# The experts' stage: 1 MB weight loads issued from Pool's queue instead of SyncE's

## The chip, the cores and the metric

The kernel runs on one core of a Trainium2 chip. The core has five engines with an instruction queue each: PE (TensorE, matrix products), DVE (VectorE), ACT (ScalarE), POOL (GpSimd) and SP (SyncE, which here only issues DMAs). DMAs that SP issues go through one hardware queue, those that Pool issues through a software queue. The metric is the device time of one execution in microseconds, lower is better.

## The reference

Three layers in a row, on a batch of 8 with 8 heads: an attention between 512 positions and 32 states per batch and head; a mixture of 8 experts, in which each of the 4352 tokens goes to one expert; and a feed-forward layer with float64 weights.

```python
def _moe_ref(x, expert_emb, tau, w1, w2):
    ...
    for e in range(E):
        mask = expert_idx == e
        h = np.maximum(x[mask] @ w1[e], 0.0)
        out[mask] = gate_w[mask, None] * (h @ w2[e])

def _moe2_ref(x, w_in, w_out, alpha):
    h = x @ w_in
    g = np.maximum(h, 0.0) + alpha * np.minimum(h, 0.0)
    return (g @ w_out).astype(np.float32)
```

D = 512, the experts' hidden width is 1024, that of the feed-forward layer 2048.

## The kernel before

Three stages follow each other: attention with routing, the experts (`moe`), the feed-forward layer (`ffn`). The profile's experts' stage lies between about 165 and 610 us.

`moe` goes through slots of 128 tokens, sorted by expert, one `step(s)` for each. The order of all instructions is written out by hand: each engine runs its own in the order in which the code emits them. Values are kept as a high and a low float16 part, so a product is three. A step does this:

- Token preparation, two steps ahead: `g_load` (L1035, Pool) gathers 128 rows by index into `xg`; `x_prep` (L138 to L140, Pool) scales them and splits them into `xs`; SP issues a DMA transpose of `xs` into `xTt` (L1041).
- First product: `mm1` (L1050, PE, 24 matmuls) reads `xTt`. `relu` splits the result into `hs` (L194 on ACT, L195 on DVE), and SP issues the DMA transpose `hT<-hs` (L1058).
- Second product: `mm2` of the step before (L1063, PE, 24 matmuls) reads `hT`. PE runs mm1(s+1) and then mm2(s), so `hT` has the time of mm1(s+1) to arrive.
- Result: `y_top` and `y_out` scale and split it into `ys` (L1070 to L1073 and L130 on DVE, L127 on ACT), Pool copies two indices (L1079) and scatters the rows to memory (L1083, `y_nat<-ys`).
- Weight swaps: where the next slot belongs to another expert (read from a table, so under branches), SP loads 2 MB of new weights into `st` in four DMAs (`swap`, L1101), and ACT and DVE convert them.

Beside this the stage prepares the feed-forward weights, which are float64. `d_load` (L1109 to L1115) brings 16 pieces of 1 MB, as pairs of int32, into `d64`, one buffer (bufs=1). `d_parts` turns a piece into float32 with three DVE instructions (`decode_ops`, L146 to L148) and then calls `d_load` for the next piece, which has to wait until the last of the three, L148, has read the buffer. The pieces are decoded in steps 2, 4, 6, 7, 8, 10, 12, 14, 18, 20 and so on to 32. `step` spreads these operations: the first runs inside `y_out`, the rest goes to `left` and runs in the next step, after `relu` and ahead of `x_prep`:

```python
            while left:
                left.pop(0)()
            ops = [op for f in work[s] for op in f()]
            ...
            if s + 2 < MS:
                x_prep(s + 2)
            y_top(s - 1)
            ...
            y_out(s - 1, fill)
            left.extend(ops)
```

Of the kernel before, what the change touches and what calls it, by code (L numbers as in the profile page):

```python
# [22 lines left out]
def tile_attn_moe_ffn(ctx, tc, x, xt, state, statet, embt, tau, w1, w2, w_in, w_out, alpha, out):  # L23


    nc = tc.nc
# [981 lines left out]
    def moe(st, winh, winl, wf, yq, yps, scp, pm, tables, order, gates):  # L1008
# [99 lines left out]
        def d_load(c):  # L1108
            d64[c] = mp.tile([128, 1024, 2], I32, tag="d64", bufs=1, name="d64")  # L1109
            if c < 8:  # L1110
                src = w_in32[(c // 2) * 128:(c // 2 + 1) * 128, (c % 2) * 2048:(c % 2 + 1) * 2048]
                nc.sync.dma_start(d64[c].rearrange("p a b -> p (a b)"), src)
            else:
                src = w_out32[(c - 8) * 256:(c - 7) * 256, :].rearrange("(k p) n -> p k n", p=128)
                nc.sync.dma_start(d64[c].rearrange("p (k a) b -> p k (a b)", k=2), src)  # L1115

        def d_parts(c):
            cs = slice((c % 8) * 1024, (c % 8 + 1) * 1024)
            ops = decode_ops(wf[:, cs], d64[c])
            if c < 15:  # L1120
                ops.append(lambda: d_load(c + 1))
            return ops
# [6 lines left out]
        d64, work = {}, {s: [] for s in range(MS)}  # L1129
# [27 lines left out]
        y_top(0)  # L1157
        y_out(0)
        d_load(0)

        left = []
# [410 lines left out]
```

## Time and profile before

| | us |
|---|---|
| median of 3 runs | 1306.46 (1304.74 to 1307.47) |
| the profiled execution | 1298.37 |
| its span | 1296.7 |
| PE busy in the span | 1209.7 (93%) |
| DVE / ACT / POOL busy in the span | 807.2 / 566.4 / 359.7 |
| DMA through SP's queue (q1) | 117.30 MB, 38.3% of 16 engines' span |
| DMA through Pool's queue (q0) | 29.49 MB, 7.8% |

The profile is of one execution. A row of the time line gives the start in us from the span's start, the duration in us, the engine (SPq is SP's queue of issues), the line of the code, the operation, what it writes and reads, how many instructions were merged into the row, and in brackets how long the engine had been idle and who ended that wait. An issuing row tells how long the issue took, not the transfer. "issue" as a releaser means that the profile shows nothing that was waited for.

### The profile page before, as it was taken

How to read it: one execution, taken by the hardware profiler on the slowest of the kernel's cores; microseconds unless marked ns; L12 is line 12 of the kernel's file. 1: busy time of each engine (PE TensorE's matmuls, PEld its weight loads, DVE VectorE, ACT ScalarE, POOL GpSimd, SP SyncE). 2: the span in 40 equal slices, each digit the busy share in tenths (PEclk: the TensorE clock that was granted, in tenths of full speed). 3: DMA queues.
4: the chain of work that ended last, by engine and by line, in shares of the span. 5: the costliest groups of instructions: out<-in, count | busy, mean ns of one | idle time of the engine just before them, and what ended most of it. 6: DMA issues, size and time to landing. Idle time of an engine off the chain costs nothing. (4 is left out here: it accounts for less than half of the span.)

```text
span 1296.7 us, 21099 instructions
## 1 busy us (share of the span) xinstructions
PE 1209.7 (93%) x7520; PEld 688.1 (53%) x7520; DVE 807.2 (62%) x1640; ACT 566.4 (44%) x1045; POOL 359.7 (28%) x421
## 2 busy tenths in 40 slices
PE   8888799898988898988899999999999999999997
PEld 5555444343333343433345666666666666666664
DVE  5898866656777776745986645645555553654543
ACT  5965532225474545443544333333433433333343
POOL 2345445544436544543302002020010202001010
PEclk9987999999989999999899999999999999999999
DMA  9984777999899999884102010020100202010000
GB/s 289 307 244 141 214 172 178 196 183 244 203 260 216 271 226 224 208 172 92 34 1 58 9 33 33 1 66 1 42 25 1 66 1 57 9 18 33 1 33 17
DMA packets 221648, 148.48 MB, mean 115 GB/s; under 512 B 174014, under 2 KB 190526, under 8 KB 220480
## 3 DMA queue, kind: packets, MB, share of 16 engines
q1 hardware_dynamic: 210976, 117.30, 38.3%
q0 software_dynamic: 10240, 29.49, 7.8%
q8 instruction: 61, 1.00, 0.3%
q14 instruction: 83, 0.68, 0.2%
q10 hardware_dynamic: 288, 0.02, 0.0%
HBM read 80.13 MB, written 28.40 MB: 84 GB/s over the span
## 5 line engine op out<-in xcount | busy, mean ns | idle before, releaser
L1386 PE MATMUL bk<-woh,arena 128*128 128x512 f16 x1088 | 391.8, 380 | 4.4 <-ACT arena L1366 2.8
L1386 PEld LDWEIGHTS <-arena 128*128 128x128 f16 x1632 | 158.5, 98 | 120.2 <-ACT arena L1366 3.1
L1386 PE MATMUL bk<-wol,arena 128*128 128x512 f16 x544 | 206.7, 380 | 0.0
L1293 POOL DMA_INDIRECT out_dram<-arena,fr x34 | 36.2, 1065 | 588.5 <-ACT arena L1391 552.0
L1446 DVE SCALAR_TENSOR_TENSOR arena<-bk,sg,arena 128x256 f32<-128x256 f32 (+1 forms) x128 | 59.7, 467 | 219.8 <-PE bk L1440 215.8
L1366 ACT CAST arena<-arena 128x512 f16<-128x512 f32 (+1 forms) x144 | 85.0, 590 | 188.7 <-DVE arena L1371 188.6
L1063 PE MATMUL yp<-w2h,hT 128*128 128x512 f16 x576 | 138.6, 396 | 29.4 <-DMA hT<-hs 21.8
L1448 ACT ACTIVATE arena<-pm,sg 128x256 f32<-128x256 f32 (+1 forms) x192 | 88.3, 461 | 158.1 <-PE pm L1440 156.8
L1063 PEld LDWEIGHTS <-hT 128*128 128x128 f16 x864 | 82.8, 100 | 137.4 <-DMA hT<-hs 35.8
L1050 PE MATMUL hp<-w1h,xTt 128*128 128x512 f16 x576 | 136.9, 389 | 15.4 <-DMA xTt<-xs 9.6
L1050 PEld LDWEIGHTS <-xTt 128*128 128x128 f16 x864 | 85.0, 99 | 124.5 <-issue 16.1
L1440 PEld LDWEIGHTS <-wS 128*128 128x128 f16 x1152 | 108.6, 98 | 52.7
L1440 PEld LDWEIGHTS <-winh 128*128 128x128 f16 x1024 | 98.0, 98 | 49.8 <-issue 2.1
L1370 DVE TENSOR_TENSOR arena<-arena 128x512 f16<-128x512 f32 (+1 forms) x144 | 94.1, 658 | 17.8 <-ACT arena L1366 17.1
L1371 DVE SCALAR_TENSOR_TENSOR arena<-arena,alpha_sb 128x512 f32<-128x512 f32 (+1 forms) x144 | 102.7, 714 | 2.9 <-ACT arena L1406 2.6
L127 ACT ACTIVATE ys<-yp,ym 128x512 f16<-128x512 f32 x38 | 26.0, 684 | 171.8 <-DVE ym L1072 157.5
L1440 PE MATMUL pm<-ysum,wS 128*128 128x256 f16 (+1 forms) x768 | 99.6, 266 | 0.0
L1083 POOL DMA_INDIRECT y_nat<-ys,pos x38 | 39.4, 1037 | 209.8 <-issue 135.4
L1440 PE MATMUL bk<-yT,winh 128*128 128x256 f16 (+1 forms) x512 | 86.5, 266 | 0.0
L1050 PE MATMUL hp<-w1l,xTt 128*128 128x512 f16 x288 | 68.4, 379 | 0.0
L1063 PE MATMUL yp<-w2l,hT 128*128 128x512 f16 x288 | 68.1, 378 | 0.1
L161 ACT ACTIVATE junk<-st 128x1024 bf16<-128x1024 f32 x56 | 59.1, 1056 | 19.4 <-SPq L1097 5.8
(318 smaller groups left out, 1904.4 us busy)
## 6 DMA issues: line engine op xcount, KB each, us to landing
st<-in_w_dram SPq DMA_DIRECT2D x64, 512.0 KB
X<-in_x_dram SPq DMA_DIRECT2D x32, 256.0 KB
d<-in_w_in_dram SPq DMA_DIRECT2D x8, 1024.0 KB
d<-in_w_out_dram SPq DMA_DIRECT2D x8, 1024.0 KB
xs_all<-xrow SPq DMA_DIRECT2D x7, 1056.0 KB
xT<-in_xt_dram SPq DMA_DIRECT2D x7, 1024.0 KB
xs_all<-xrow SPq DMA_DIRECT2D x2, 528.0 KB
xT<-in_xt_dram SPq DMA_DIRECT2D x2, 512.0 KB
```

Of the source, the lines that this page charges most:

```text
L161: nc.scalar.activation(out=junk, in_=W[i][0][:, c, :], func=AF.Square, accum_out=fsq[i][:, c:c + 1])
L1050: nc.tensor.matmul(hp[s][c], lhsT=xTt[s][:, q + k, :], rhs=wt[:, k, c * 512:(c + 1) * 512], start=(i == 0 and k == 0), stop=(i == 2 and k ...
L1063: nc.tensor.matmul(yp[s], lhsT=hT[s][:, q + k, :], rhs=wt[:, k, :], start=(i == 0 and k == 0), stop=(i == 2 and k == KE - 1))
L1083: nc.gpsimd.indirect_dma_start(out=y_nat[:], out_offset=bass.IndirectOffsetOnAxis(ap=pos[:, s:s + 1], axis=0), in_=ys[:].bitcast(I32), in_ ...
L1293: nc.gpsimd.indirect_dma_start(out=out, out_offset=bass.IndirectOffsetOnAxis(ap=fr[g][:, t, 2:3].bitcast(U32), axis=0), in_=src, in_offset ...
L1366: nc.scalar.copy(slot[G[g, m]][:, 0, 0:n], h)
L1370: tt(d[:, 1, 0:n], h, d[:, 0, 0:n], sub)
L1371: return [lambda: nc.vector.scalar_tensor_tensor(h, in0=h, scalar=alpha_sb[:, m:m + 1], in1=h, op0=ALU.mult, op1=ALU.max), hi, lo]
L1386: nc.tensor.matmul(ps, lhsT=slot[G[g, m]][:, lg, t * 128:(t + 1) * 128], rhs=wo[lw][:, m, :], start=(m == order[0] and i == 0), stop=(m == ...
L1440: nc.tensor.matmul(ps, lhsT=a, rhs=b, start=(i in (1, 2, 5) and j == 0), stop=(j == len(ops) - 1), skip_group_check=True)
L1446: nc.vector.scalar_tensor_tensor(d, in0=ps, scalar=sc, in1=d, op0=ALU.mult, op1=add)
L1448: nc.scalar.activation(out=d, in_=ps, func=AF.Copy, scale=sc)
```

## The change

The two lines that issue the 16 loads of `d64` name another engine's queue. Nothing else in the code is changed; the place in the code at which a load is called stays.

```diff
@@ -1109,10 +1109,10 @@
             d64[c] = mp.tile([128, 1024, 2], I32, tag="d64", bufs=1, name="d64")
             if c < 8:
                 src = w_in32[(c // 2) * 128:(c // 2 + 1) * 128, (c % 2) * 2048:(c % 2 + 1) * 2048]
-                nc.sync.dma_start(d64[c].rearrange("p a b -> p (a b)"), src)
+                nc.gpsimd.dma_start(d64[c].rearrange("p a b -> p (a b)"), src)
             else:
                 src = w_out32[(c - 8) * 256:(c - 7) * 256, :].rearrange("(k p) n -> p k n", p=128)
-                nc.sync.dma_start(d64[c].rearrange("p (k a) b -> p k (a b)", k=2), src)
+                nc.gpsimd.dma_start(d64[c].rearrange("p (k a) b -> p k (a b)", k=2), src)
```

The order of SP before the change, at the eleventh load (the one of the time line's 407.26 us): the load, the transpose of the tokens, under a branch four loads of weights, the transpose of the hidden tile.

```order
686 L1115 DMA d_5297<-in_w_out_dram 128x2x1024
687 L1095 UNCONDITIONAL_BRANCH
688 L1105 UNCONDITIONAL_BRANCH
689 L1041 DMA_TRANSPOSE xTt_2266<-xs_2264 128x8x128
690 L113 TENSOR_LOAD tab
691 L1097 COMPARE_AND_BRANCH
```

After the change SP's rows at that place begin with the transpose.

```order
676 L1095 UNCONDITIONAL_BRANCH
677 L1105 UNCONDITIONAL_BRANCH
678 L1041 DMA_TRANSPOSE xTt_2266<-xs_2264 128x8x128
679 L113 TENSOR_LOAD tab
680 L1097 COMPARE_AND_BRANCH
```

The load has gone from between the branches; what follows on SP stands in the same order as before.

Pool before the change, from the preparation of the tokens (`xs_2264`) that this transpose reads, to the store and the gather that follow.

```order
378 L138 TENSOR_TENSOR xg_2261<-xg_2261 128x512
379 L139 CAST xs_2264<-xg_2261 128x512
380 L140 TENSOR_TENSOR xs_2264<-xg_2261,xs_2264 128x512
381 L1079 COPY ys_2274<-ids 128x2
382 L1090 UNCONDITIONAL_BRANCH
383 L1095 UNCONDITIONAL_BRANCH
384 L1105 UNCONDITIONAL_BRANCH
385 L1097 UNCONDITIONAL_BRANCH
386 L1095 UNCONDITIONAL_BRANCH
387 L1105 UNCONDITIONAL_BRANCH
388 L1083 DMA y_nat<-ys_2274,pos 4352x528
389 L1035 DMA xg_2258<-xs_all,idx 128x528
```

Pool after the change, the same stretch.

```order
392 L1115 DMA d_5297<-in_w_out_dram 128x2x1024
393 L1095 UNCONDITIONAL_BRANCH
394 L1105 UNCONDITIONAL_BRANCH
395 L138 TENSOR_TENSOR xg_2261<-xg_2261 128x512
396 L139 CAST xs_2264<-xg_2261 128x512
397 L140 TENSOR_TENSOR xs_2264<-xg_2261,xs_2264 128x512
398 L1079 COPY ys_2274<-ids 128x2
399 L1083 DMA y_nat<-ys_2274,pos 4352x528
400 L1035 DMA xg_2258<-xs_all,idx 128x528
```

The load, and with it the wait for DVE's L148, now stands on Pool ahead of the three instructions that make `xs_2264`, which SP's transpose waits for; the copy, the store and the gather follow. It is so at fifteen of the sixteen loads; the first has no decode ahead of it.

## Rows read from the trace of the kernel before

**Rows 1.** Busy time by stage (stretch, us, each engine, PE clock, DMA share, GB/s)

```profile
165.00:610.00 445.00, 400.11 (x1795) 174.41 (x1793) 299.03 (x536) 198.70 (x301) 215.23 (x225) 0.97 0.91 205
```

**Rows 2.** Waits of PE, 165 to 610 us (total, times, longest)

```profile
PE yp L1063 <- DMA hT<-hs: 21.8, 10, 4.5
PE hp L1050 <- DMA xTt<-xs: 9.6, 5, 4.1
```

**Rows 3.** Time line of DVE, 402 to 413 us

```profile
403.88 2.03 DVE L147 SCALAR_TENSOR_TENSOR wf<-d,c_top,wf 128x1024 int32<-128x1024 int32 x1 [1.48 <-DVEq L1095]
405.95 1.28 DVE L148 SCALAR_TENSOR_TENSOR wf<-d,c_sh,wf 128x1024 int32<-128x1024 int32 x1
...
409.03 0.75 DVE L130 SCALAR_TENSOR_TENSOR ys<-yp,ym,ys 128x512 f16<-128x512 f32 x1 [0.64 <-ACT ys L127]
```

**Rows 4.** Time line of SP's issues, 195 to 520 us

```profile
199.08 1.87 SPq L1058 DMA_TRANSPOSE hT<-hs  x1
...
300.96 0.36 SPq L1112 DMA_DIRECT2D d<-in_w_in_dram  x1
301.97 1.62 SPq L1041 DMA_TRANSPOSE xTt<-xs  x1
...
382.06 0.41 SPq L1115 DMA_DIRECT2D d<-in_w_out_dram  x1
382.64 1.25 SPq L1041 DMA_TRANSPOSE xTt<-xs  x1
385.70 3.68 SPq L1101 DMA_DIRECT2D st<-in_w_dram  x4
390.93 3.57 SPq L1058 DMA_TRANSPOSE hT<-hs  x1
...
407.26 0.40 SPq L1115 DMA_DIRECT2D d<-in_w_out_dram  x1
407.84 1.26 SPq L1041 DMA_TRANSPOSE xTt<-xs  x1
411.87 3.28 SPq L1058 DMA_TRANSPOSE hT<-hs  x1
...
507.17 1.29 SPq L1041 DMA_TRANSPOSE xTt<-xs  x1
```

**Rows 5.** Time line of PE, 195 to 520 us

```profile
203.49 3.63 PE L1063 MATMUL yp<-w2h,hT 128*128 128x512 f16 x16
...
259.27 5.31 PE L1063 MATMUL yp<-w2h,hT 128*128 128x512 f16 x16 [3.67 <-DMA hT<-hs]
...
318.26 5.16 PE L1063 MATMUL yp<-w2h,hT 128*128 128x512 f16 x16 [4.46 <-DMA hT<-hs]
...
397.72 3.63 PE L1063 MATMUL yp<-w2h,hT 128*128 128x512 f16 x16 [2.91 <-DMA hT<-hs]
...
413.65 1.18 PE L1050 MATMUL hp<-w1h,xTt 128*128 128x512 f16 x4 [0.17 <-DMA xTt<-xs]
...
421.45 3.63 PE L1063 MATMUL yp<-w2h,hT 128*128 128x512 f16 x16 [0.92 <-DMA hT<-hs]
...
513.98 3.62 PE L1050 MATMUL hp<-w1h,xTt 128*128 128x512 f16 x16
```

**Rows 6.** Time line of POOL, 399 to 414 us

```profile
401.87 1.05 POOL L138 TENSOR_TENSOR xg<-xg 128x512 f32<-128x512 f32 x1
...
403.68 1.16 POOL L140 TENSOR_TENSOR xs<-xg,xs 128x512 f16<-128x512 f32 x1
...
410.56 1.03 POOL L1083 DMA_INDIRECT y_nat<-ys,pos  x1 [4.60 <-DVE ys L130]
411.89 0.98 POOL L1035 DMA_INDIRECT xg<-xs_all,idx  x1 [0.30 <-issue]
```

**Rows 7.** POOL's gathers and its one plain DMA (ns min/median/max, first and last start)

```profile
L1035 POOL DMA_INDIRECT xg<-xs_all,idx x40: 946/982/1034, 156.4 to 607.1; - x40
L281 POOL DMA_DIRECT2D xs_all<-srow x1: 822/822/822, 12.7 to 12.7; - x1
```

## The prediction

> **What bounds the kernel now.** I went from the page to the stage, then to its waits, then to one step of it on five engines. In the experts' stage TensorE is busy for 400.1 of 445 us [rows 1], so time there is TensorE's, and only what makes TensorE wait costs anything. The table of waits names what it waits for: ten times the transposed hidden tile `hT` (21.8 us) and five times the transposed tokens `xTt` (9.6 us) [rows 2]. Both are DMA transposes that SP issues, one after the other, in a fixed order. So the change matters through two questions: when SP can issue `xTt` and `hT`, and how long they then travel.
>
> The step with the load at 407.26 shows how tight this is. On VectorE the last decode, L148, ends at 405.95 + 1.28 = 407.23 and frees the buffer [rows 3]. SP, held until then, issues the load at 407.26, `xTt` at 407.84 and `hT` at 411.87, when VectorE has finished the hidden tile [rows 3, 4]. TensorE waits 0.17 us for that `xTt` until 413.65 and 0.92 us for that `hT` until 421.45 [rows 5]. `xTt` behind the load thus travels 5.8 us, `hT` 9.6 us. Pool in that step prepares the tokens from 401.87 to 403.68 + 1.16 = 404.84 and then sits idle for 4.60 us before it issues the store [rows 6]: the preparation is early and hidden.
>
> **What the change takes away.** On SP, 16 issues of about 0.4 us and the wait for L148 ahead of them [rows 4]. This is worth little by itself, as `xTt`, next on SP, still has to wait, now for Pool. On SP's DMA queue, 1 MB ahead of `xTt`. What does a transpose cost with nothing ahead? The `hT` issued at 199.08 is in use at 203.49: 4.4 us [rows 4, 5]. `xTt` is half as large; I take 3.5 us, bounded by 4.4 above and about 3 below (half of the 4.4 would be movement at most, an estimate), and 5.8 if it goes on meeting other traffic.
>
> **What it adds on Pool.** The load now stands ahead of the token preparation L138 to L140, and waits for L148. Costs from that moment: Pool's DMA starts late after a wait, as the store does (wait over at 409.03 + 0.75 = 409.78 [rows 3], start at 410.56 [rows 6]): 0.78 us. Then the issue: 0.82 us for the one plain DMA that Pool issues, 0.95 to 1.03 for the 40 gathers [rows 7]; I take 1.0, as the load has 128 rows like a gather. Then the preparation, 2.97 us (401.87 to 404.84). `xTt` goes out at 407.23 + 0.78 + 1.0 + 2.97 + 0.05 = 412.0 instead of 407.84: 4.2 us later, and with 3.5 us instead of 5.8 to travel it lands 1.9 us later. Fifteen loads stand so; the first has no decode ahead of it.
>
> Who feels it? Ten of the fifteen have several us until TensorE wants `xTt`, or belong to the next paragraph. Five are tight. In the step shown nothing is left; in the last of the five `xTt` was issued at 507.17, landed by the same 5.8 us at 513.0, and TensorE began with it, without a wait, at 513.98 [rows 4, 5]: 1.0 us left. With 0.9 left on average, five steps lose 1.0 each: **+5.0 us**.
>
> `hT` stands behind `xTt` on SP. SP needs 1.25 us to issue `xTt` and 1.8 us of branches and table reads (382.64 + 1.25 to 385.70 [rows 4]; 1.55 from the last weight load to `hT`). With 1.6, `hT` could go at 412.0 + 1.25 + 1.6 = 414.9, 3.0 us later than now. But its 9.6 us of travel are a collision: Pool issues the gather at 411.89, 0.02 us after `hT` [rows 4, 6], and the two share the DMA engines; without it 4.4 us are enough. After the change store and gather follow the preparation at once (412.5 and 413.8), about 1 us ahead of `hT`, and should mostly be through. I take 5.8 us, between 4.4 and 9.6: `hT` lands at 420.7. TensorE, 2 us late from `xTt`, wants it 24 matmuls later, at 16 in 3.63 us: 415.5 + 5.4 = 420.9. So the `hT` waits of these steps go: four, the first 3.67 us (until 259.27), with 0.92 in the step shown; 6.4 us together. The first also slowed TensorE: the 16 matmuls after it took 5.31 us where 16 take 3.63 [rows 5], 1.7 us more. **-8.1 us**.
>
> **Three loads with a weight swap behind them.** In three steps SP issues 2 MB of the next expert's weights between `xTt` and `hT`. There the 4 us are not absorbed: load at 382.06, `xTt` 382.64, weights 385.70 to 389.38, `hT` 390.93, for which TensorE waits 2.91 us until 397.72 [rows 4, 5]. With `xTt` at 382.06 + 4.8 = 386.85, weights and `hT` go out 4.1 us later, on the same queue in the same order, so TensorE starts 4.1 us later. Its wait becomes 7.0 us, longer than the 3.67 us that was followed by slow matmuls, which adds 1.7: +5.8. In the first of the three the load goes out at 300.96 and `xTt` only at 301.97, after a preparation that overlapped the decode [rows 4]; the new time, 300.96 + 4.8 = 305.8, is 3.8 us later, less up to 0.9 as the overlap ends, and the wait of 4.46 us already has the slow matmuls (5.16 [rows 5]): +2.9. The third I put at +1.8, an estimate from the first, since its preparation overlaps the decode too and SP is held up there by a swap ahead of the load as well. **+10.5 us**.
>
> **Sum.** 5.0 - 8.1 + 10.5 = +7.4 us. The profiled execution took 1298.37 us (span 1296.7), so 1305.8 for such a one. The median of the runs shown, 1306.46, lies 8.1 above it; carried over, 1306.46 + 7.4 = **1314 us**. The later store, gather and 1 MB landing cost nothing by my reading: their results are used one or two steps later, and a step is 48 matmuls, 10.9 us at 16 in 3.63.
>
> **Rivals.** *Faster.* The collision goes (-8.1) and the lateness is absorbed. For this speaks that Pool's preparation and VectorE's decode would no longer overlap: L147 took 2.03 us in the step shown, under the preparation, and L148, an instruction of the same form, 1.28 [rows 3], so the decode would end up to 0.8 us sooner. If `xTt` travels 3.0 us, the five steps lose (4.2 - 0.8 - 2.8 - 0.9, under zero) nothing. It decides if the three swap steps also lose less than 2 us each: -8.1 + 3 = -5, 1301 us. Against it: those three waits are a plain chain on SP. Chance 0.23.
>
> *No change.* SP saves its issues, Pool's idle 4.60 us swallows the preparation, and the three swap steps cost what the collision gives back: 1306 us. The Trainium skill supports this outcome (DMA: Bandwidth & Descriptors, section "Issuing engines are not separate DMA queues"): DMAs run on the same 16 engines whoever issues them, so moving an issue saves only the sequencer's own time. By that the sum would be nil, as SP's 16 issues are off the path. Chance 0.17.
>
> *Much slower.* Packets of Pool's queue between those of a transpose stretch it, as the gather does now (9.6 us against 4.4). If load tail, store and gather now do that to `xTt`, it travels 5.8 us again and lands 4.2 later: five steps lose 3.3 each, 16.5, and the `hT` waits stay (no -8.1): 16.5 + 10.5 = +27, 1333 us. Half of that is as likely as all. Chance 0.15.
>
> *Starved issue.* If VectorE holds up Pool while it issues, 1.0 us becomes 1.0 plus a VectorE instruction, 0.75 (L130) to 2.03 us (L147) [rows 3]. Over the five tight steps and three swap steps that is 6 to 16 us more: 1320 to 1330. The 40 gathers, all within 0.95 to 1.03 us beside a busy VectorE [rows 7], speak against it. The Trainium skill warns of it (SBUF — State Buffer, section "Who interferes with whom"): a DMA from Pool's queue can stall because VectorE starves its descriptor generation, and one from SP cannot. By the gathers' rows, this case's trace does not agree so far. Chance 0.07.
>
> **Chances.** My forecast, +3 to +14 us (1309 to 1321), 0.38. A measurement of this kernel tells about 0.2% (2.6 us) from no change. Faster 0.23, within 0.2% 0.17, slower 0.38 + 0.15 + 0.07 = 0.60. The range leaves out about one in ten on each side: 1298 to 1329.
>
> **What would show it.** Right: `xTt` about 4 us later after L148 in each of the 15 steps, Pool idle before the load and not before the store, waits for `xTt` up by some 5 us, waits for `hT` down except in the three swap steps, where they grow. Wrong: `xTt` at its old place, or waits for `hT` as long as now in the other steps; a Pool issue much over 1 us; or `xTt` travelling 5.8 us although the load is off its queue.

## The result and the profile after

| | before | after |
|---|---|---|
| median of 4 runs | 1305.6 us (1303.17 to 1307.47) | 1320.99 us (1318.75 to 1327.64) |
| ratio, 95% interval | | 1.0127 [1.0084, 1.0171] |
| profiled execution, its span | 1298.37, 1296.7 | 1323.19, 1321.5 |

The change makes the kernel 1.3% slower: 15.4 us between the medians, where +7.4 was forecast. The time lies inside the range, the sign is right, the size is about double.

The traffic moved as the diff says: the page's part on the queues has 100.52 MB through SP's queue (117.30 before) and 46.27 MB through Pool's (29.49).

The waits of PE after, from 165 to 640 us (total, times, longest), beside [rows 2]:

```profile
PE yp L1063 <- DMA hT<-hs: 36.2, 9, 9.8
PE hp L1050 <- DMA xTt<-xs: 10.1, 6, 3.4
PE yp L1063 <- ACT hs L194: 8.1, 1, 8.1
...
PE yp L1063 <- ACT ys L127: 2.2, 1, 2.2
```

The third row is an `hT` wait too. The view names the releaser that came last by its records, and ACT's part of `hs` was long done: the matmuls in question start at 407.82, the moment at which an `hT` lands (below). The fourth is of the same kind: its matmuls start at 375.23, and the `hT` of 363.51 lands 11.7 us after its issue. Before there were two such by their place, the first matmul that reads a new `hT`, which the prediction's 21.8 left out; from the same view of the kernel before:

```profile
PE yp L1063 <- DVE w2l L130: 4.9, 1, 4.9
...
PE yp L1063 <- ACT ys L127: 2.3, 1, 2.3
```

So PE waited 46.5 us for `hT` where it was 29.0, and for `xTt` 10.1 where it was 9.6. The tokens, which go out late, cost almost nothing where they are used; the hidden tile pays.

Now the step that the prediction showed. Time line of DVE after, the last decode:

```profile
417.01 1.30 DVE L148 SCALAR_TENSOR_TENSOR wf<-d,c_sh,wf 128x1024 int32<-128x1024 int32 x1
```

Time line of POOL after, there and at the first swap step (L1112 and L1115 are the load):

```profile
295.42 0.57 POOL L1112 DMA_DIRECT2D d<-in_w_in_dram  x1 [2.18 <-DVE wf L148]
...
305.49 1.07 POOL L1083 DMA_INDIRECT y_nat<-ys,pos  x1 [5.05 <-issue]
306.87 0.97 POOL L1035 DMA_INDIRECT xg<-xs_all,idx  x1 [0.30 <-issue]
...
418.61 0.75 POOL L1115 DMA_DIRECT2D d<-in_w_out_dram  x1 [6.86 <-DVE wf L148]
419.38 1.06 POOL L138 TENSOR_TENSOR xg<-xg 128x512 f32<-128x512 f32 x1
...
421.19 1.15 POOL L140 TENSOR_TENSOR xs<-xg,xs 128x512 f16<-128x512 f32 x1
```

Time line of SP's issues after, at the two swap steps and at the step shown:

```profile
302.37 2.70 SPq L1101 DMA_DIRECT2D st<-in_w_dram  x4
305.99 6.77 SPq L1058 DMA_TRANSPOSE hT<-hs  x1
...
393.23 2.31 SPq L1101 DMA_DIRECT2D st<-in_w_dram  x4
396.79 6.88 SPq L1058 DMA_TRANSPOSE hT<-hs  x1
...
422.37 1.26 SPq L1041 DMA_TRANSPOSE xTt<-xs  x1
```

L148 ends at 418.31; Pool, idle for 6.86 us, issues the load 0.30 later in 0.75, prepares the tokens until 422.34, and `xTt` goes out at 422.37, 4.1 us after L148. That is the forecast chain.

PE after, at the matmuls that waited (in brackets) or that matter here; 16 of these take 3.63 us:

```profile
182.60 3.63 PE L1063 MATMUL yp<-w2h,hT 128*128 128x512 f16 x16 [3.09 <-DMA hT<-hs]
...
299.83 3.63 PE L1063 MATMUL yp<-w2h,hT 128*128 128x512 f16 x16 [0.18 <-DMA hT<-hs]
...
320.15 5.53 PE L1063 MATMUL yp<-w2h,hT 128*128 128x512 f16 x16 [9.76 <-DMA hT<-hs]
...
407.82 6.06 PE L1063 MATMUL yp<-w2h,hT 128*128 128x512 f16 x16 [8.08 <-ACT hs L194]
...
451.57 3.63 PE L1063 MATMUL yp<-w2h,hT 128*128 128x512 f16 x16 [2.28 <-DMA hT<-hs]
...
463.68 3.63 PE L1063 MATMUL yp<-w2h,hT 128*128 128x512 f16 x16 [1.56 <-DMA hT<-hs]
...
487.89 5.29 PE L1063 MATMUL yp<-w2h,hT 128*128 128x512 f16 x16 [2.57 <-DMA hT<-hs]
...
526.60 6.40 PE L1063 MATMUL yp<-w2h,hT 128*128 128x512 f16 x16 [5.26 <-DMA hT<-hs]
```

The two longest waits are those of the first two swap steps, as forecast: 9.76 us where it was 4.46, and 8.08 where it was 2.91 [rows 5]. The third swap step is the one whose second product starts at 463.68; PE waited 1.56 us there, and 1.42 before (below). Most of the others are new. How long the transfers behind the two longest travelled stands in the view of the tile (issue: duration in ns, first and last start; then time from issue to landing, us). They are, after, the `hT` of 305.99 and the `hT` of 396.79:

```profile
L1058 SPq DMA_TRANSPOSE hT<-hs x1: 6769/6769/6769, 306.0 to 306.0; - x1
DMA to landing us min/median/max: 14.1/14.1/14.1
...
L1058 SPq DMA_TRANSPOSE hT<-hs x1: 6880/6880/6880, 396.8 to 396.8; - x1
DMA to landing us min/median/max: 11.0/11.0/11.0
```

Before, the same two `hT` were in use 7.1 and 6.8 us after their issue (311.19 by the trace of before, and 390.93 [rows 4], to 318.26 and 397.72 [rows 5]). So `hT` travels up to twice as long. How late it goes out is read against the second product (`mm2`) of the step before, which starts at 299.83 ahead of the first of the two, and before at 303.25. PE before, at that product and at the third swap step:

```profile
303.25 3.62 PE L1063 MATMUL yp<-w2h,hT 128*128 128x512 f16 x16
...
448.50 3.63 PE L1063 MATMUL yp<-w2h,hT 128*128 128x512 f16 x16 [1.42 <-DMA hT<-hs]
```

Time line of SP before, the `hT` of the first swap step:

```profile
311.19 5.11 SPq L1058 DMA_TRANSPOSE hT<-hs  x1
```

In the first swap step `hT` thus goes out 6.2 us behind the start of that product, where it was 7.9 before. It is not late at all, and the longer wait is all travel. One reason that it is not late is that DVE's decode no longer overlaps Pool's preparation there: L147 and L148 took 2.85 and 1.51 us before and 1.28 each after. In the second, `hT` goes out 9.5 us behind the product that starts at 387.30, where it was 7.0 us (390.93, behind 383.98): 2.5 us later, and 4.2 us longer on the way.

What the `hT` of 305.99 meets can be read from the issues and landings. The last of the weights are there at 313.0, when ACT, which waits for them, goes on. Then this `hT`, the gather of 306.87 and the next `xTt` (313.87) are in flight. From 312 to 315 us and from 315 to 318 us the DMA engines move 77 and 97 GB/s at a share of 1.23 and 1.12 (the sum of the packets' times, which passes 1 where they overlap); the stage before has 205 at 0.91 [rows 1]. The gather lands after 12.6 us, where the median is 4.9, and `hT` 0.6 us behind it.

From its first matmul to the first of the next stage, the experts' stage is 25.7 us longer in the profiled execution (177.35 to 608.46 before, 174.16 to 630.96 after). Of these, 17.5 us are `hT` waits, 0.5 `xTt` waits and 6.8 slow matmuls (last section), 24.8 in all. The two executions lie 24.8 apart too (1298.37, 1323.19), as the stage ahead ended 3.2 us sooner and the one behind took 2.3 longer. That is more than the 15.4 between the medians, as the one of before was a short one by 7.2 us and the one of after a long one by 2.2.

### The profile page after: what moved, and what is told of

Its sections match the earlier page's. It is cut to its first block, busy times and chain, and to the rows that moved or that the text cites. A ratio compares the mean times of both kernels' runs of the same rounds, so it can differ in the third digit from the quotient of the medians.

```text
span 1321.5 us, 21079 instructions
## 1 busy us (share of the span) xinstructions
PE 1216.0 (92%) x7520; PEld 688.8 (52%) x7520; DVE 796.2 (60%) x1640; ACT 567.2 (43%) x1045; POOL 356.1 (27%) x437
## 3 DMA queue, kind: packets, MB, share of 16 engines
q1 hardware_dynamic: 207648, 100.52, 34.5%
q0 software_dynamic: 13568, 46.27, 11.2%
## 5 line engine op out<-in xcount | busy, mean ns | idle before, releaser
L1063 PE MATMUL yp<-w2h,hT 128*128 128x512 f16 x576 | 144.7, 409 | 47.3 <-DMA hT<-hs 36.2
L1050 PE MATMUL hp<-w1h,xTt 128*128 128x512 f16 x576 | 137.4, 391 | 14.2 <-DMA xTt<-xs 10.1
L1050 PEld LDWEIGHTS <-xTt 128*128 128x128 f16 x864 | 85.2, 99 | 124.5 <-issue 15.4
```

The costliest lines, as they stand in the source:

```text
L1050: nc.tensor.matmul(hp[s][c], lhsT=xTt[s][:, q + k, :], rhs=wt[:, k, c * 512:(c + 1) * 512], start=(i == 0 and k == 0), stop=(i == 2 and k ...
L1063: nc.tensor.matmul(yp[s], lhsT=hT[s][:, q + k, :], rhs=wt[:, k, :], start=(i == 0 and k == 0), stop=(i == 2 and k == KE - 1))
```

## The experiments

Each ran beside the kernel before on one chip; the ratio is against that. Single executions of one kernel lie up to 1% and more apart, so an interval is about 0.4% (5 us) wide to each side. The three sets had medians of 1308.8, 1307.4 and 1308.2 for the kernel before.

| kernel | queue of the loads | Pool waits for L148 ahead of the tokens | median, us | ratio, 95% |
|---|---|---|---|---|
| changed, again | Pool | yes | 1328.2 | 1.0137 [1.0083, 1.0190] |
| load behind the tokens | Pool | no | 1320.7 | 1.0106 [1.0068, 1.0144] |
| Pool, two buffers | Pool | no | 1331.7 | 1.0148 [1.0099, 1.0196] |
| wait alone | SP | yes | 1314.5 | 1.0021 [0.9979, 1.0062] |
| SP, two buffers | SP | no | 1301.3 | 0.9968 [0.9936, 1.0000] |
| three swap loads on SP, 13 on Pool | both | at 12 | 1307.3 | 0.9982 [0.9942, 1.0021] |
| first load alone on SP | both | yes | 1317.4 | 1.0053 [1.0014, 1.0092] |
| three swap loads on Pool, 13 on SP | both | at 3 | 1320.7 | 1.0093 [1.0059, 1.0126] |
| wait alone at the three | SP | at 3 | 1316.4 | 1.0075 [1.0029, 1.0121] |
| three on Pool, behind the tokens | both | no | 1313.0 | 1.0041 [1.0005, 1.0078] |
| changed, gather ahead of the store | Pool | yes | 1311.1 | 1.0052 [1.0017, 1.0087] |
| SP, two buffers, gather ahead | SP | no | 1282.8 | 0.9844 [0.9790, 0.9898] |

My theory was the prediction's: the place on Pool costs, since the load's wait for L148 holds up the tokens. The rival was the queue: the load's packets now run between those of SP's transposes.

**The load behind the tokens.** The changed kernel; each load is issued after `x_prep`.

```diff
-                ops.append(lambda: d_load(c + 1))
+                ops.append(lambda: pend.append(c + 1))
...
                 x_prep(s + 2)
+            while pend:
+                d_load(pend.pop(0))
```

> The loads stay on Pool's queue, but each is issued behind the token preparation of its step, no longer ahead of it. Theory (the place on Pool is what costs: the load's wait for L148 holds up the preparation, so xTt goes out 4 us late, and the weights of a swap and hT behind it): xTt goes out as early as in the kernel before, the waits for hT in the three swap steps fall from 8 to 10 us to under 5, and the time is 1298 to 1309 against 1306 for the kernel before. Rival (the queue costs: the load's packets on Pool's queue run between those of the transposes and stretch them): the waits stay, at least 1315 as in the changed kernel (1321).

1320.7 us: the theory fails here. Tokens no longer wait for L148, and the time stays that of the changed kernel; the three swap steps still have `hT` waits of 6.09, 6.55 and 5.84 us. The rival's mechanism shows where SP issues `xTt` at 278.32 and Pool the load at 278.59 (view of the tiles):

```profile
L1041 SPq DMA_TRANSPOSE xTt<-xs x1: 1247/1247/1247, 278.3 to 278.3; - x1
DMA to landing us min/median/max: 9.2/9.2/9.2
...
L1112 POOL DMA_DIRECT2D d<-in_w_in_dram x1: 606/606/606, 278.6 to 278.6; - x1
DMA to landing us min/median/max: 10.4/10.4/10.4
```

The `hT` and the gather ahead of them had landed by 278.2, and the next issue is Pool's store at 281.91, so at first these two have only each other. In the changed kernel the loads of its eight `w_in` and eight `w_out` pieces land in the median after 6.1 and 5.5 us (view of the DMA issues). And there an `xTt` issued when the load is nearly through, as at 422.37, lands after 3.0. This run alone does not separate the two: it takes one cost away and puts the other in.

**The wait alone.** The kernel before, with a tiny copy on Pool.

```diff
-                ops.append(lambda: d_load(c + 1))
+                ops.append(lambda: (nc.gpsimd.tensor_copy(pw, wf[:, cs][:, 1023:1024]), d_load(c + 1)))
```

> The kernel before, loads on SyncE's queue, with one tiny copy on Pool (128x1) at the place where the changed kernel has its load: it reads what L148 has written, so the preparation waits for L148 with no load on Pool's queue. Theory (the wait on Pool is the larger part): xTt goes out about 3.5 us later after L148 than before, behind the load on the same queue, and the three swap steps show hT waits of 7 to 10 us; 1312 to 1328. Rival (queue): 1303 to 1309, since nothing is moved to Pool's queue. One thing can only be seen here: if it is slower than the changed kernel (1321), the change of queue itself gives something back.

1.0021, and by the medians +5.7 us, at the lower edge of what the theory expected. The interval takes in 1, so a cost of the wait over all the loads is not shown; the changed kernel's interval starts above the end of this one's, so it is not the whole loss. Of the three swap steps the first shows the forecast wait, 9.07 us, as in the changed kernel; the others have 4.37 and 1.59 us. That `hT`, too, goes out no later than before (6.7 us behind the second product ahead of it) and is in use only 12.9 us after its issue.

**The three swap loads back on SP.**

```diff
-                nc.gpsimd.dma_start(d64[c]...
+                (nc.sync if c in (7, 9, 11) else nc.gpsimd).dma_start(d64[c]...
```

> The changed kernel, with the three loads that have a weight swap behind them back on SyncE; thirteen stay on Pool. Theory (three swap steps are the bulk of the loss; by the two traces they show +5, +4 and +9 us at the steps of 303, 385 and one between or behind): 1304 to 1311, and the hT waits of 9.76 and 8.08 us become about 4.5 and 3. If the twelve other loads on Pool cost as my forecast says (+5 for xTt, -8 for hT) it ends a little under the kernel before, 1303. Rival (every load on Pool costs about the same, by its packets): a fifth of the loss comes back, 1317 to 1319.

0.9982: no loss is left, with thirteen loads still on Pool. The two waits are 3.63 us at 316.30 and 3.31 at 400.54, about as expected.

**The first load back on SP** (`c == 0` in the same place).

> The changed kernel, with the first load alone, which has no decode ahead of it, back on SyncE. In the changed kernel it is issued 0.6 us behind an hT transpose, that transpose takes 7.6 instead of 4.3 us and TensorE waits 3.1 us for it. Theory: this is the load's packets between those of the transpose, with no wait on Pool in play; back on SyncE the wait of 3.1 us is gone and the time is 2 to 4 us lower, 1317 to 1319. Rival (the attention stage ahead shifted, and the load has nothing to do with it): the wait stays, 1321.

The wait at the first load is gone from the trace, and the median is 3.6 us below the changed kernel's, as expected. The ratio, 1.0053, would say more, but its interval overlaps that of the changed kernel; the changed kernel's second profile had only 0.84 us of this wait. What the first load costs is not shown beyond this.

**The changed kernel again.**

> The changed kernel once more, beside the others of this set, since single executions of either kernel lie up to 1% apart. Both theories expect what it gave: 12 to 16 us above the kernel before, 1318 to 1324. A second profile tells which of its hT waits repeat: by the theory (tokens late on SyncE's queue) the two of the swap steps near 320 and 408 us, 8 to 10 us each, and the 3 us wait at the first load; the waits near 452, 488, 527 and 540 us, if they depend on when a gather meets a transpose, need not be there.

1.0137; the median, 1328.2, is above the expected 1318 to 1324. The first two swap waits repeat, slightly shorter than expected (7.40 us at 317.20, 7.98 at 406.74), and the third swap step now has 6.63 at 465.87. The first load's wait shrinks to 0.84. Of the later ones, that of 526.60 comes again at the same step (7.18 until 532.59); those of 451.57 and 487.89 do not.

**The reverse: only the three swap loads on Pool** (`c not in (7, 9, 11)` above).

> The reverse of the experiment that put three loads back: only the three loads with a weight swap behind them go through Pool, thirteen stay on SyncE. Theory (these three carry the loss): 1316 to 1324, at least 8 us above the kernel before, with hT waits of 7 to 10 us in those steps. Rival (the loss is in all sixteen loads, and putting any three back would have shortened it by luck of where gathers fall): under 1312.

1.0093, +12 to +13 us: with the run of three loads back on SP this shows that these three carry most of the loss. Their `hT` waits are 7.28, 3.87 and 7.84 us, so the second stays below the 7 to 10 expected. By the prediction's terms the other loads would come to 5.0 - 8.1 = -3.1; their run's 0.9982 (-2.4 us, interval -8 to +3) fits that.

**Two buffers, on Pool and on SP.** `tag="d64", bufs=2` in place of `bufs=1`, in the changed kernel and in the kernel before. Where the load stands is left as it was.

> The changed kernel with two buffers for the loaded pieces: the load stands at the same place on Pool, but its buffer has long been free, so Pool does not wait for L148 there and only the issue (0.6 to 0.8 us) stands ahead of the token preparation. Theory (the wait costs): xTt at most 0.8 us later than in the kernel before, the three swap steps back at hT waits of 3 to 5 us, 1300 to 1310. Rival (packets of Pool's queue beside a transpose cost, as in the experiment with the preparation first, 1321): the load meets the transposes now as then, 1315 to 1325.

> The kernel before with two buffers for the loaded pieces: SyncE does not wait for L148, the load goes out ahead of xTt as soon as SyncE is there. The partner of the run with two buffers on Pool: the two differ in the queue alone. Theory (the queue itself costs little): both within 5 us of each other, this one 1298 to 1309. Rival (the queue costs): this one is at least 8 us below its partner.

1.0148 against 0.9968: with no wait for L148 in either, the change of queue makes 1.8%, some 24 us; on Pool, 1331.7 is above even the rival's range. This refutes the theory as the main cause for the sixteen loads together. The two differ in the queue alone as they are written; in the traces the moment of the issue differs with it. On Pool 13 of the 16 loads go out between 0.8 us ahead of an `hT` and 2.0 us behind it. On SP none does: the nearest goes out 3.0 us behind one. What a load at Pool's moments would cost on SP's own queue, no run shows. The waits of PE for `hT` from 165 to 640 us, with two buffers on Pool:

```profile
PE yp L1063 <- DMA hT<-hs: 60.7, 15, 12.5
```

The same view with two buffers on SP:

```profile
PE yp L1063 <- DMA hT<-hs: 32.1, 12, 5.8
```

The longest travel on Pool's side is around the load at 462.99 and the `xTt` at 467.50 (views of the tiles):

```profile
L1115 POOL DMA_DIRECT2D d<-in_w_out_dram x1: 776/776/776, 463.0 to 463.0; - x1
DMA to landing us min/median/max: 17.8/17.8/17.8
...
L1041 SPq DMA_TRANSPOSE xTt<-xs x1: 6290/6290/6290, 467.5 to 467.5; - x1
DMA to landing us min/median/max: 14.0/14.0/14.0
```

The load takes three times its usual 5.5 us, `xTt` over four times 3.0, and SP is held 6.29 us by the issue of it. These two are not alone: the `hT` of 461.08, which takes 19.7 us to land, and the gather of 462.01 went out just ahead.

The Trainium skill says of this (DMA: Bandwidth & Descriptors, section "Queues, rings and completion order") that each DMA engine goes round-robin, packet by packet, between the queues that have work. That the two share the engines agrees with these rows; how long each then takes is the runs' to say.

**The two costs at the three swap loads.** The wait alone there, loads on SP (the tiny copy only where `c + 1 in (7, 9, 11)`), and the queue alone (these three on Pool, behind the tokens).

> The kernel before, with the tiny copy on Pool that waits for L148 ahead of the preparation at three loads alone, those with a weight swap behind them; all loads stay on SyncE. With the run that moved only these three to Pool (+12 us) and the next one it separates, at these three steps, the late tokens from the load's queue. Theory of the order (late tokens hold the weights and hT on SyncE): most of the 12 us, 1314 to 1322, hT waits of 7 to 10 us there. Theory of the queue (packets of Pool's queue beside those of SyncE's): 1303 to 1310.

> The kernel before, with the same three loads on Pool's queue but issued behind the token preparation, so the tokens go out as early as before and only the queue is changed. Theory of the order: 1303 to 1310. Theory of the queue: 1312 to 1322, with the load and the transposes issued beside it each taking 8 to 14 us to land. If both this run and the one with the wait alone lose, the two costs stand in for each other; if neither does, they are needed together.

1.0075 and 1.0041, against 1.0093 with both. PE's waits from 300 to 480 us, in the kernel before:

```profile
PE yp L1063 <- DMA hT<-hs: 11.6, 6, 4.5
PE hp L1050 <- DMA xTt<-xs: 5.2, 3, 2.8
```

With both costs (three loads on Pool):

```profile
PE yp L1063 <- DMA hT<-hs: 26.4, 7, 7.8
PE hp L1050 <- DMA xTt<-xs: 8.0, 4, 2.8
```

With the wait alone:

```profile
PE yp L1063 <- DMA hT<-hs: 19.2, 6, 6.9
PE hp L1050 <- DMA xTt<-xs: 6.4, 2, 3.5
```

With the queue alone:

```profile
PE yp L1063 <- DMA hT<-hs: 16.0, 6, 6.0
PE hp L1050 <- DMA xTt<-xs: 11.2, 3, 8.3
```

With what the view puts to ACT (2.3 us before, then 0, 0.9 and 0.5), these are 19.1 us of waits before, 34.4 with both, 26.5 with the wait alone and 27.7 with the queue alone. The last holds one that the three loads explain at most in part: the `xTt` issued at 423.89 ends a wait of 8.31 us at 434.77 (2.82 before), and PE had been idle for 5.1 us of it when the nearest of the three, the load of 431.56, went out. At the `hT` of the three swap steps themselves PE waited 8.8 us before (4.46, 2.91 and 1.42), 13.9 with the wait alone (6.90, 4.49 and 2.52), 11.2 with the queue alone (5.96, 2.05 and 3.22) and 19.0 with both.

So by the times each costs something by itself. But late tokens do not cost by a late `hT`: with the wait alone, too, the `hT` of the first two swap steps go out no later than before (6.9 and 7.0 us behind the second product ahead, where it was 7.9 and 7.0) and are in use 10.6 and 9.1 us after their issue instead of 7.1 and 6.8. Which of the two costs is the larger, and whether they add up, the intervals and these single profiles don't tell; the profile with both is of the longest of its kernel's runs (1330.4, median 1320.7).

**The gather ahead of the store**, in the kernel with two buffers on SP and in the changed one. Without the edit, Pool issues the gather within 0.1 us of many an `hT` in both (10 and 6 times; as at 396.79 above).

```diff
                 x_prep(s + 2)
+            if s + 4 < MS:
+                g_load(s + 4)
...
             left.extend(ops)
-            if s + 4 < MS:
-                g_load(s + 4)
```

> The kernel with two buffers on SyncE (1301), and Pool's gather issued right behind the token preparation, ahead of the store, so that it no longer meets hT. If an hT that takes 8 to 12 us does so because a gather is issued within about 0.1 us of it, most hT travel falls to 4.4 to 6 us, the hT waits in total from 32 to under 18 us, and the time is 1282 to 1296. If the store or the weights do it, or the gather only moves to xTt: 1298 to 1306.

> The changed kernel with the gather ahead of the store, as in the run beside it. Theory (in the swap steps the late tokens put hT where it meets the gather, and this is the part of the loss that was forecast too small): the hT waits near 320 and 408 us fall from 8 to 10 us to about 5 to 7, the time by 6 to 15 us to 1306 to 1315. If the load itself or the late weights make all of it: 1318 to 1326.

1282.8 us (0.9844, the lower edge of what was expected), and 1311.1 (1.0052, where the changed kernel has 1.0127 and 1.0137). PE's waits for `hT` in the faster one, from 165 to 640 us:

```profile
PE yp L1063 <- DMA hT<-hs: 16.2, 8, 4.0
```

A step to see it in. Time line of POOL before, a gather:

```profile
247.19 0.98 POOL L1035 DMA_INDIRECT xg<-xs_all,idx  x1 [0.30 <-issue]
```

Time line of SP before, the `hT` that goes out 0.04 us ahead of it; PE waits 3.67 us for this one, until 259.27 [rows 5]:

```profile
247.15 3.21 SPq L1058 DMA_TRANSPOSE hT<-hs  x1
```

Time line of POOL in the faster kernel, the same step:

```profile
253.17 1.30 POOL L1035 DMA_INDIRECT xg<-xs_all,idx  x1 [0.15 <-issue]
```

Time line of SP in the faster kernel:

```profile
251.23 3.01 SPq L1058 DMA_TRANSPOSE hT<-hs  x1
```

Now the gather comes 1.9 us after `hT`, and PE does not wait at this step. The place of the gather alone is worth 1.2% here (0.9968 to 0.9844, two kernels on SP that differ in nothing else), and this kernel is the fastest of all. In the changed kernel with the same edit the row of `hT` waits falls from 36.2 to 19.0 us; the wait at 398.64 is still 6.60, one of 6.14 at 455.41 is put to ACT's queue, and the `xTt` waits rise from 10.1 to 16.7. At the first swap step the wait falls from 9.76 to 2.88 us (315.56), so most of that one went with the gather.

That the collision with the gather is a part of the loss does not follow from the times, though: the same edit gains about 10 us in the changed kernel and 16 in the one on SP. The collision costs both, and with the gather moved the two lie 2.1% apart (0.9844 and 1.0052; they differ in the buffers too).

## Why the prediction was right in sign and half in size

- **The chain on Pool** was right to a few tenths: start 0.30 us after L148 (0.78 forecast), issue 0.56 to 0.77 (1.0), preparation 2.96 (2.97), `xTt` 4.1 us after L148 (4.8), travel 3.0 behind a load that is nearly through (3.5). At the second and third swap step the preparation took 4.2 us, and `xTt` went out 5.3 us after L148. Pool idles before the load, not before the store, at eleven of the fifteen steps. No load shows an issue starved by VectorE, so that rival is out for them; one gather, at 478.49, took 1.83 us to issue instead of 0.98.
- **Five tight steps, +5.0 us**, was too much: the `xTt` waits rose from 9.6 to 10.1 us in all. In the step shown `xTt` lands 3.0 us after 422.37, at 425.4, and no wait for it is listed.
- **The `hT` waits that go, -8.1 us**: three of the four went (those that ended at 259.27, 341.96 and 421.45); the fourth, 1.03 us until 470.47, came back as 2.57 until 487.89. But others appeared in steps that I had taken as free: 3.09 us at the first load, 2.28 at 451.57, whose `hT` the third swap load follows by 0.08 us (440.69 and 440.77), and 5.26 at 526.60 (0.38 before).
- **Three swap steps, +10.5 us**: the place was right, the chain was not. The first two waits went from 4.46 to 9.76 and from 2.91 to 8.08 (+5.3 and +5.2, the second +2.4 more for slow matmuls, 6.06 instead of 3.63); forecast were +2.9 and +5.8. But "weights and `hT` go out 4.1 us later" held for `hT` in neither: against the second product ahead of it, it went out 1.8 us earlier in the first and 2.5 us later in the second. I let `hT` travel as long as before; it took 14.1 and 11.0 us instead of 7.1 and 6.8. In the second, `hT` goes out behind the weights and beside a gather; in the first, beside a store, with the gather 0.88 us behind (305.99 and 306.87). In both, `hT` also follows the first weight load more closely, by 3.6 us instead of 5.6 and 5.2; no run separates this from the gather. The third, forecast at +1.8, shows no loss in this profile (1.42 before, 1.56 after), but 6.63 in the repeat; ahead of its load, at 432.42, SP was held by the issue of an `hT` (428.26, 2.95 us) and not, as I wrote, by a swap. Moved alone, these three loads cost 0.93%, 12 us, so +10.5 came close, but by another way than the one I gave: in part that is luck.
- **The step that failed** beside that chain is the sentence "The later store, gather and 1 MB landing cost nothing by my reading". It looked only at who uses their results. What they do to the transposes that run beside them, on the other queue, was priced at nothing, and the two runs that differ in the queue, and in the moments of issue that come with it, put that at 1.8%. What I priced comes closest to the kernel with the wait alone: 1.0021, +2.7 us (-2.7 to +8.1), which just takes in +7.4. The changed kernel is about 14 us above it.
- **The rivals.** *Much slower* (0.15) named the missing mechanism, packets of Pool's queue that stretch transposes, but put it on `xTt`; it fell on `hT` and on the swap steps, and part of the -8.1 came, so 1321 lies between it and the forecast. *No change* (0.17) had with it the Trainium skill (DMA: Bandwidth & Descriptors, section "Issuing engines are not separate DMA queues"), by which the choice of the issuing engine saves only issue time. The runs differ from that, if it is read as a rule for time: the same 16 MB through the other queue cost 1.1 to 1.8% here. *Faster* failed on the swap steps, as was held against it, though by travel more than by the plain chain.
- **Open**: how the swap steps' loss divides between late tokens and queue (0.75% and 0.41%, overlapping), and how late tokens lengthen the travel of an `hT` that is not late itself; whether it is the other queue or the moment of issue that costs the 1.8%; why the changed kernel (1.0127, 1.0137) seems above the sum of its two parts (1.0093 and 0.9982), which the intervals allow to be chance; and what the first load costs beyond its 3 us wait.

## What to carry to other kernels

Moving a transfer to another queue is no move to other wires: it also takes away the order that one queue gave. Here a load and a transpose that stood behind each other on one queue ran against each other on two, and took up to three and nearly five times as long. So price a moved DMA by what is in flight beside it, above all transposes on the critical path, and not only by the engine that issues it. And before moving loads, look at which short transfers are issued at the same instant as a critical one: here shifting one gather by a few us was worth more (1.2%) than any placing of the loads that was tried.

## What the runs showed of the hardware that was not expected

- A 1 MB load on Pool's queue beside SP's transposes: 10.4 us for the load and 9.2 for `xTt` where at first only the two meet, 17.8 and 14.0 with an `hT` and a gather in flight as well, against 5.5 to 6.1 and 3.0 apart.
- An `hT` and a gather that meet: 14.1 and 12.6 us at 305.99 and 306.87, while the engines moved 77 to 97 GB/s.
- SP is held while its transposes are stretched: the issue of one took 6.29 to 6.88 us in the rows above, 1.25 to 1.87 in the shorter of [rows 4]. What stands behind it on SP is late too.
- Slow matmuls weigh as much as some waits. In nine places of the stage after, the 16 matmuls behind a wait took 5.29 to 6.55 us, 20.0 us more together than at 3.63 each (the first at 320.15, the last, of 5.57, at 623.82); before there were eight, 13.2 us more (the first at 259.27 [rows 5], the last, of 4.97, at 601.92).
  The granted clock tells why (busy time of these stretches after, clock third from the right):

```profile
182.60:186.20 3.60, 3.60 (x18) 1.70 (x19) 2.07 (x4) 0.00 (x0) 0.00 (x0) 1.00 0.56 91
...
487.89:493.18 5.29, 5.29 (x18) 2.10 (x19) 4.74 (x4) 3.64 (x4) 0.00 (x0) 0.68 0.86 242
```

  1.00 is 2.4 GHz; 0.68 is a mean over a part at 1.2 and a part at 2.4. PE had been idle for 3.09 us before the stretch that stayed at 1.00, and for 2.57 before the other, so the length of the wait alone does not decide it.
